# A long convolution by a two-stage Fourier transform: adjacent PSUM writes in the inverse, and a last stage in 32 × 32 tiles

## The chip, the cores and the metric

The kernel runs on one core of a Trainium2 chip. The time is the device time of one execution in microseconds, the median over several runs. The core has five engines with a queue of instructions each: TensorE (PE in the profile, and PEld for its weight loads), VectorE (DVE), ScalarE (ACT), GpSimd (POOL) and SyncE (SP), which here issues most of the DMAs. They wait for each other by semaphores only.

## The reference, cut to what matters

```python
x  = A_u                                    # 1 x 2048 x 512, bf16
xn = layernorm(x)
K  = real(sum over n of C * exp(dt*A*l) * dt*B)      # a filter of length 2048 for each of 512 channels
y  = irfft(rfft(xn, 4096) * rfft(K, 4096))[:2048]    # a causal convolution along the sequence
s  = y + xn * Dskip
g  = silu(xn + scatter_add(one row, a small gated MLP of that row))
return x + s * g
```

The convolution of 2048 positions for 512 channels is most of the work. The change touches only its last part: the product of the two spectra, the inverse transform, and the final `x + s * g`.

## The kernel before

The transform of length 4096 is done as two stages of small dense transforms on TensorE. A frequency is k2 + 64·k1 (32 values of k2, 64 of k1), a position is l1 + 64·l2 (64 values of l1, 32 of l2). Channels are split in two halves `h` of 256, and a half into four groups `q` of 64 channels `m`.

First come the layer norm, the forward transform of the input (`useq`, `useq2`), which goes through a DRAM scratch `scr_u`, and the generation of the filters from the parameters (`kgen_*`), a long chain on DVE. `kgen_kx` (L1057, stage kx1 for the second half) ends with KX, the filter at 640 sample points. Then, for each half:

- `load_u` (L1117) brings the spectrum of the input back into `UU[h]`, with the (real, imaginary) pair of k1 on the 128 partitions and `[t, q, k2, m]` along them; t = 1 is the same with the two parts swapped. For the second half the t = 1 copy is made by 8 copies on DVE or ScalarE (L1130, L1131).
- `spec` (L1137): for each of 16 pairs of k2, ten matmuls of 256 columns turn KX into the filter's spectrum in a PSUM bank (two banks alternate), `evac` copies it to `KF`, and DVE multiplies. For `h = 0` one instruction of 128 × 1024 multiplies UU in place. For `h = 1` four instructions of 128 × 256 write the products to another buffer `Y1`, whose innermost index is four channels.
- `inv_a` (L1160): the first inverse stage, from k1 to l1. Eight operations `x8` take eight channels m each; a channel is two matmuls (t = 0, 1) whose weights are the 128 values (q, k2) of that channel and whose 128 moving columns are the tables FA1 and FA2. The output of a channel goes to every fourth float of a bank (`pr.a.reshape(2, 128, 4)[i // 4, :, i % 4]`). Two pairs of banks alternate. Four copies of 64 partitions × 512 then bring (q, k2) × (part, l1) × m into `C`, so that the part lies on the upper or lower half of the partitions beside two of the four q, and the channels are adjacent.
- `fin_h` (L1203): the second inverse stage, from k2 to l2, and the end. For each l1 and q a matmul with 128 rows: the weights are a 128 × 32 table `FB` that holds zeros for the other q of the pair, the moving operand is 64 columns of C. The four values of l1 that lie 16 apart go to the four column strips of 32 (position `(0, 32 * a)`). ScalarE copies a group of rows to TB, DVE multiplies TB by G and adds it to XR (the input rows), and, for the second half only, four DMAs store the rows. The groups are 4, 4, 4, 4 values of l1 for `h = 0` and 4, 4, 4, 2, 2 for `h = 1`. In the last four rows a small matmul with VM (4 rows, table E127) first writes a correction.

`ldg` loads G (2 MB from scratch), `fpre` applies SiLU to it in four instructions of 128 × 2048 on ScalarE; `ldz` loads FB (1 MB), `ldr` the input rows XR.

In the program the order is spec0, inv0, loads and fpre, fin_h(0), spec1, inv1, fin_h(1). What each engine does in which order, though, is written out by hand: every operation has a number in the order of the program, the table `ORDER` lists the numbers for each of the five engines, and `_Graph.schedule` and `emit` only add the waits that follow from reads and writes. An operation made by `flex` or `evac` can stand in ScalarE's or in DVE's list. The `cost` arguments don't act in this kernel, since the order is given. In the old table fin_h(0) stands on TensorE in four pieces between the last spec1 operations and those of inv1 and its last piece behind inv1.

Of the kernel before, what the change touches and what calls it, by code (L numbers as in the profile page):

```python
# [340 lines left out]
def tables():  # L341
# [28 lines left out]
    FZ = np.zeros((2, 2, 32, 64, 2, 32))  # L370
    for q in range(2):
        FZ[:, q, :, :, q] = FB.transpose(2, 0, 1, 3)
    FB = FZ.reshape(128, 64, 2, 32)
# [6 lines left out]
        9 8 10 3-4 19 14 13 20 16 15 216 18 212 17 214 148 144 149-150 146 102 97 100 151 147 101 99 143 142 96 145 95 98 155 157 154 156 152-153 222  # L380
        224 218 220 226 228 230 232 236 238 234 240 250 252 242 254 316 256 258 321 260 708 264 262 326 331 709 336 268 341 270 266 346 710 351 711
        713-714 278 712 851 808 804 806-807 803 805 1006 1005 1004 1014 1016 1015 1025 1028 1026 1003 1052 1017 1027 1038 1051 1041 1040 1039""",
    scalar="""
        2 6 5 7 12 11 21 53-54 22 29 55 26 25 30 24 27 57-59 46 450 440 425 34 31 33 444 38 446 435 48 426 452 454 443 424 37 442 439 430 136 449 88
# [4 lines left out]
        592 579 597 578 575 340 338 500 598-599 570 628 577 590 587 574 588 600 345 343 514 576 520 581 348 518 350 595 586 522 596 582 524 584 572  # L389
        528 530 532 534 672 716 719 722 725 639 728 731 643 641 734 737 645 743 740 749 746 755 686 688 761 752 690 758 692 854 698 696 764-765 771  # L390
        700 769-770 776 775 704 777 781-782 786 811-812 789 792 790 879 810 873 794 891 801 885 809 897 802 915 909 797 927 921 939 933 951 823 945
        830 957 959-960 837 963 969 968 972 975 977 980 984 983 989 988 992 848 993 1000 1011 1022 1035 1048 1053-1054""",
    vector="""
        0-1 211 105 103 106 113 104 111 66 71 28 112 107 109 23 117 56 110 62-63 108 118 68 114 65 116 115 64 61 119 36 67 60 70 69 120 32 72 121 73
        122 74 123 75 84 124 76 125 77 126 78-79 127 131 80 128 81 129 82 130 132 83 133-134 85 137-139 86 135 140-141 87 91 90 92-93 89 94 161 164
        159 167 170 173 362 360 364 179 359 367 283 368 184-185 361 186 369 363 373 457 374 188 379 456 376 459 380 190 458 191-193 460 462 385 195
        461 388 464 463 197 466 198-200 465 375 467-468 202 469-472 386 473 205 474 476 475 210 477-478 274-275 479-482 309 484 488 485 506 486-487
        490 489 505 483 503 491-492 244 247 494 493 507 498 245 508 330 496 509-510 246 335 249 203 511-512 603 606 604 607 605 609 516 608 610-611
        671 613 612 615 614 616-617 619 618 673 621 630 620 622-623 625 624 626-627 526 629 631 633 632 272 635 276 634 277 674 636-637 646-647 649
        648 650-654 656 655 658 657 535 660 659 662 661 664 663 676 666 665 675 668 667 670 669 678 677 679-680 682 681 684 683 729 741 726 732 717  # L400
        747 735 744 762 720 738 723 759 753 750 756 857 694 853 766-767 855 859 772 774 706 858 702 852 707 779 784 780 787 785 867 791 871 861 856
        862-863 796 814 880-881 870 883 865 882 868 864 818 875 869 816 876 795 894 892 874 877 815 903 895 817 905 887 906 886 889 888 799 898 800
        900-901 899 893 912 904 913 910 930 911 907 925 929 924 922 916 941 940 942 918 917 923 934 931 919 928 943 937 953 955 954 952 936 824 935
        946 948 947 949 825 831-832 958 964 962 965 967 970 974 973 979 978 982 985 987 990 994 838 995 839 849-850 1001-1002 1012-1013 1023-1024
        1049-1050 1036-1037""",
    gpsimd="""
        447 390 389 536-537 42 39 41 40 43-44 594 279""",
    tensor="""
        45 47 158 160 163 166 162 169 165 172 168 171 175 178 174 181 49 177 282 51 180 183 286 187 290 280 189 294 284 194 298 196 288 302 201 292
        204 306 296 206-209 310 300 213 215 217 304 219 221 223 308 225 227 229 231 314 312 233 235 319 317 237 324 239 322 241 243 327 497 329 495  # L410
        332 501 334 499 337 339 515 344 251 253 255 519 342 513 349 347 257 259 517 261 263 521 525 523 527 529 531 533 265 267 269 271 715 718 721
        724 638 727 730 642 640 733 736 644 742 739 748 745 754 685 687 760 751 689 757 691 697 695 693 763 768 699 773 705 701 703 778 783 860 866
        788 813 793 878 872 798 890 884 902 896 914 908 926 920 938 932 950 819-822 944 826-829 956 961 833-836 966 840 842 841 843-845 971 976 981
        986 991 846-847 996-999 1007-1010 1018-1019 1031 1020-1021 1032 1029-1030 1033-1034 1044-1045 1042-1043 1046-1047""",
# [7 lines left out]
def build(nc, A_u, A_A_re, A_A_im, A_B_re, A_B_im, A_C_re, A_C_im, A_log_dt, A_Dskip,  # L422
# [52 lines left out]
    with g.ctx:  # L475
# [73 lines left out]
        C = apart("C", RM, RM2, [2, 64, 64])  # L549
        Y1 = g.buf("Y1", RQ0, [2, 16, 4, 32, 4], BF16)  # L550
# [29 lines left out]
        def cost(eng, v, rate):  # L580
            return FIX[eng] + v.n * rate
# [43 lines left out]
        def evac(out, in_):  # L625
            g.op(AC, lambda e: e.activation(out=out.ap, in_=in_.ap, func=ACT.Copy), w=[out], r=[in_], cost=cost(AC, out, 0.71) + 80,  # L626
                 alt=(DV, lambda e: e.tensor_copy(out=out.ap, in_=in_.ap), cost(DV, out, 1.05) + 95))  # L627

        def evac_a(out, in_):
            g.op(AC, lambda e: e.activation(out=out.ap, in_=in_.ap, func=ACT.Copy), w=[out], r=[in_], cost=cost(AC, out, 0.71))  # L630
# [506 lines left out]
        def spec(h, kps, fd, k0):  # L1137
            uu, kx = UU[h], KX[h]
            for n_, kp in enumerate(kps):
# [11 lines left out]
                if h == 0:  # L1151
                    uv = uu(uu.a[:, :, 2 * kp:2 * kp + 2].reshape(2, 4, 128))
                    tt(DV, uv, uv, kf(bc(kf.a[None], (2, 4, 128))), ALU.mult)
                else:
                    for kk in range(2):
                        for t in range(2):
                            k2 = 2 * kp + kk
                            tt(DV, Y1(Y1.a[t][:, :, k2].transpose(1, 0, 2)), uu(uu.a[t, :, k2].reshape(4, 16, 4)), kf(kf.a[:, 64 * kk:64 * kk + 64].reshape(4, 16, 4)), ALU.mult)
# [22 lines left out]
        inv_a(0)  # L1181
        g.stage = "ldz"
# [17 lines left out]

        nt = 0

        def fin_h(h):  # L1203
            nonlocal nt
            g.stage = f"fin{h}"
            for kb, (r0, nr) in enumerate(((0, 4), (4, 4), (8, 4), (12, 4)) if h == 0 else ((0, 4), (4, 4), (8, 4), (12, 2), (14, 2))):
                pr = PP[0 if h == 0 else kb % 2]
                bk = [PB[(0 if h == 0 else 2 * (kb % 2)) + k] for k in range(2)]
                blk = lambda q: bk[q // 2](bk[q // 2].a[64 * nr * (q % 2):64 * nr * (q % 2) + 64 * nr])
                for q in range(4):  # L1210
                    if r0 >= 12:
                        mm([(blk(q), CB(cb("E127")[0:128], 0, 4), VM(VM.a.reshape(4, 4, 2, 64)[r0 - 12:r0 - 12 + nr, q, h], 0, 4), q % 2 == 0, None, None)], 160)
# [81 lines left out]
```

## Time and profile before

| what | value |
|---|---|
| median of 3 runs | 220.25 us (219.12 to 220.3) |
| profiled execution | 220.46 us |
| its span, first to last instruction | 218.6 us |
| mean granted TensorE clock | 0.813 |
| copies of C | 30 on DVE, 34 on ScalarE |
| stores | 18 on SP, 2 on ScalarE |

A row of the profile names an engine, a line of the kernel (often that of a helper: L647 is every matmul, L626 and L627 every `evac` on ScalarE and on DVE, L598 every product of tensors), the buffers as out<-in, the shape as partitions × elements, and a count. In rows that group instructions, busy time and the mean duration in ns follow, then the idle time of the engine just before them and what ended it. In rows by time, the first number is the start in us from the start of the span, the second the length from the first start to the last end. In a table by stretches each engine has its busy time and number of instructions, then come the granted clock, the share of the DMA engines and GB/s. PB is any PSUM bank, and 128*64 on a matmul is rows times columns of the weights.

### The profile page before, as it was taken

How to read it: one execution, taken by the hardware profiler on the slowest of the kernel's cores; microseconds unless marked ns; L12 is line 12 of the kernel's file. 1: busy time of each engine (PE TensorE's matmuls, PEld its weight loads, DVE VectorE, ACT ScalarE, POOL GpSimd, SP SyncE). 2: the span in 40 equal slices, each digit the busy share in tenths (PEclk: the TensorE clock that was granted, in tenths of full speed). 3: DMA queues.
4: the chain of work that ended last, by engine and by line, in shares of the span. 5: the costliest groups of instructions: out<-in, count | busy, mean ns of one | idle time of the engine just before them, and what ended most of it. 6: DMA issues, size and time to landing. Idle time of an engine off the chain costs nothing.

```text
span 218.6 us, 6958 instructions
## 1 busy us (share of the span) xinstructions
PE 166.0 (76%) x2995; PEld 134.7 (62%) x2995; DVE 189.4 (87%) x408; ACT 161.3 (74%) x318; POOL 13.8 (6%) x17
## 2 busy tenths in 40 slices
PE   0150787799868768879957499989999997999440
PEld 0140676573654346657746488889889886988330
DVE  3999988998999999999999999476779999767970
ACT  2899999999999999999722144464689977556630
POOL 2021430000000000000000620000000000000000
PEclk9995555555965559999988799997999999999755
DMA  6990579700455896969999972059980000000076
GB/s 216 396 374 0 138 142 200 294 3 0 151 178 175 232 352 177 308 179 264 310 286 213 363 294 108 3 126 390 208 240 3 3 0 4 3 0 3 3 199 187
DMA packets 21142, 36.76 MB, mean 168 GB/s; under 512 B 1944, under 2 KB 16888, under 8 KB 20088
## 3 DMA queue, kind: packets, MB, share of 16 engines
q1 hardware_dynamic: 20120, 35.60, 54.2%
q10 hardware_dynamic: 960, 0.72, 1.0%
q8 instruction: 23, 0.38, 0.7%
q14 instruction: 7, 0.06, 0.1%
q0 software_dynamic: 32, 0.00, 0.0%
HBM read 25.83 MB, written 8.39 MB: 157 GB/s over the span
## 4 chain that ended last, share of the span: by engine, by line
PE 41%; DVE 35%; ACT 13%; issue 5%; DMA 2%; SPq 0%; DVEq 0%
PE PB L647 41%; DVE TT L598 8%; DVE QQ L598 8%; DVE Y L598 4%; DVE GG L598 3%; ACT E L593 2%; DMA X<-in_A_u_dram 2%; DVE ST L760 2%; ACT AU L626 2%; ACT TB L593 2%; ACT SL L593 2%; DVE LST L616 1%; ACT XT L626 1%; DVE QQ L1024 1%; ACT QQ L593 1%
## 5 line engine op out<-in xcount | busy, mean ns | idle before, releaser
L647 PE MATMUL PB<-KX,FD 128*128 128x256 bf16 x320 | 38.7, 281 | 0.0
L647 PEld LDWEIGHTS PB<-KX,FD 128*128 128x128 bf16 x320 | 31.6, 101 | 5.8 <-ACT KX L626 0.4
L647 PE MATMUL PB<-QQ,GG 128*20 128x42 bf16 x1024 | 25.0, 263 | 9.7 <-DVE QQ L598 5.2
L647 PEld LDWEIGHTS PB<-QQ,GG 128*20 128x20 bf16 x1024 | 21.4, 124 | 13.5 <-issue 6.8
L627 DVE CAST C<-PB 64x512 bf16<-64x512 f32 x30 | 20.7, 689 | 9.5 <-PE PB L647 8.2
L626 ACT ACTIVATE C<-PB 64x512 bf16<-64x512 f32 x34 | 20.1, 592 | 11.9 <-PE PB L647 10.7
L626 ACT ACTIVATE KF<-PB 128x512 bf16<-128x512 f32 x29 | 17.3, 598 | 13.7 <-PE PB L647 12.9
L598 DVE TENSOR_TENSOR TT<-GG,MB 128x2048 bf16<-128x2048 bf16 (+3 forms) x32 | 24.3, 787 | 0.3
L593 ACT ACTIVATE QQ<-TH 128x256 bf16<-128x256 f32 x64 | 22.5, 427 | 0.0
L593 ACT ACTIVATE E<-AR 128x256 bf16<-128x256 f32 x64 | 22.3, 426 | 0.0
L598 DVE TENSOR_TENSOR QQ<-QQ,E 128x1024 bf16<-128x1024 bf16 (+2 forms) x16 | 19.6, 1252 | 0.0
L647 PE MATMUL PB<-CB,XZN 32*128 32x64 bf16 x256 | 15.8, 327 | 4.4 <-ACT AU L626 3.5
L647 PEld LDWEIGHTS PB<-CB,XZN 32*128 32x128 bf16 x256 | 12.8, 203 | 7.0 <-ACT AU L626 5.0
L647 PE MATMUL PB<-CB,UU 128*128 128x128 bf16 x128 | 17.0, 338 | 0.0
L626 ACT ACTIVATE KE<-PB 128x336 bf16<-128x336 f32 x13 | 6.0, 464 | 13.7 <-PE PB L647 13.7
L647 PE MATMUL PB<-AU,F2U 64*128 64x256 bf16 x128 | 12.6, 342 | 4.4 <-ACT UST L626 3.6
L647 PEld LDWEIGHTS PB<-CB,UU 128*128 128x128 bf16 x128 | 15.7, 185 | 0.4 <-issue 0.2
L598 DVE TENSOR_TENSOR GG<-TT 128x1024 bf16<-128x1024 bf16 (+3 forms) x38 | 15.1, 434 | 0.4
L647 PE MATMUL PB<-CB,Y 128*128 128x128 bf16 x128 | 14.6, 313 | 1.1 <-DVE Y L598 1.1
L626 ACT ACTIVATE AU<-PB 128x1024 bf16<-128x1024 f32 x14 | 14.2, 1041 | 0.5 <-PE PB L647 0.5
L647 PEld LDWEIGHTS PB<-CB,Y 128*128 128x128 bf16 x128 | 13.5, 137 | 1.6 <-DVE Y L598 1.2
L598 DVE TENSOR_TENSOR Y<-UU,KF 128x256 bf16<-128x256 bf16 x64 | 14.0, 283 | 0.4 <-ACT KF L626 0.3
(133 smaller groups left out, 287.5 us busy)
## 6 DMA issues: line engine op xcount, KB each, us to landing
FD<-c_fd SPq DMA_DIRECT2D x4, 1280.0 KB, 7.6
scr_u<-UST SPq DMA_DIRECT2D x8, 512.0 KB, 5.2
UU<-scr_u SPq DMA_DIRECT2D x2, 2048.0 KB, 15.4
XZN<-XN SPq DMA_DIRECT2D x16, 128.0 KB, 4.2
scr_g<-XN SPq DMA_DIRECT2D x4, 512.0 KB, 7.2
UU<-scr_u SPq DMA_DIRECT2D x2, 1024.0 KB, 11.3
XR<-in_A_u_dram SPq DMA_DIRECT2D x4, 512.0 KB, 14.6
G<-scr_g SPq DMA_DIRECT2D x1, 2048.0 KB
```

Source lines behind the costliest of these rows:

```text
L593: g.op(AC, lambda e: e.activation(out=out.ap, in_=in_.ap, func=func, **kw), w=[out], r=r, cost=cost(AC, out, 0.71), table=table, tokr=tokr ...
L598: g.op(eng, lambda e: e.tensor_tensor(out=out.ap, in0=a.ap, in1=b.ap, op=op), w=[out], r=[a, b], cost=cost(eng, out, rate))
L616: g.op(eng, lambda e: e.scalar_tensor_tensor(out=out.ap, in0=a.ap, scalar=x, in1=b.ap, op0=op0, op1=op1), w=[out], r=r, cost=cost(eng, out ...
L626: g.op(AC, lambda e: e.activation(out=out.ap, in_=in_.ap, func=ACT.Copy), w=[out], r=[in_], cost=cost(AC, out, 0.71) + 80, alt=(DV, lambda ...
L627: alt=(DV, lambda e: e.tensor_copy(out=out.ap, in_=in_.ap), cost(DV, out, 1.05) + 95))
L647: ins = e.matmul(o_.ap, lhsT=l_.ap, rhs=r_.ap, start=st, stop=sp, **kw)
L760: g.op(DV, lambda e, b=b: e.bn_stats(ST6(ST6.a[b]).ap, X0(X0.a[b]).ap), w=[ST6(ST6.a[b])], r=[X0(X0.a[b])], cost=620)
L1024: lambda e: e.tensor_scalar(out=out.ap, in0=in_.ap, scalar1=-1.0, scalar2=None, op0=ALU.mult), cost(DV, out, 0.3))
```

## The change

The program becomes: spec0, inv0, spec1, inv1, loads and fpre, then one last stage for both halves.

- In `inv_a` a channel's output goes to 128 adjacent floats, for both halves from UU; `Y1` is gone, and in `spec` both halves multiply UU in place.
- One copy per `x8` brings all 128 partitions × 1024 elements to C and swaps channel and (part, l1) on the way: it reads PSUM with a step of 128 floats and writes eight adjacent channels. Only the last one of the second half is split in two. C is now `[h, part, l1, m]` on partitions (q, k2), and its second half lies where UU0 was.
- The second inverse stage is undivided by half: `FB` is the bare table, repeated on four strips of 32 partitions. For each l1, part and q a matmul of 32 rows × 32 columns of weights and 128 moving columns (both halves) goes to position `(32 * q, 32 * a)`, and the two parts accumulate. Each q has its own bank. There are 512 such matmuls, as there were of the old kind.
- Row groups of the last stage are 2, 4, 4, 2, 2, 2 values of l1 for both halves together, each with two copies, products and adds of 128 × 256 nr elements; the last product of all is taken by DVE straight from PSUM in two pieces. There are 24 stores instead of 20, 2 of them on ScalarE.
- `ORDER` is a new table throughout. The work before spec0's inverse is the same set of operations in another order, and some movable ones change engine. TensorE now does the end of the second half's filters with the first two inverse operations between, then inverse operations of the first half between those of spec1, the last two of them behind spec1, then inv1 and the last stage (group 1 before group 0). ScalarE has the copies of inv0's operations 0, 1, 6, 7 and of inv1's 0 to 5 and half of 7, DVE the others. Three of the four SiLU instructions stand on ScalarE between spec1's copies 0 and 5, the fourth before copy 6. SP loads G, FB and XR in this order instead of XR, G, XR, XR, FB, XR.

```diff
-    FZ = np.zeros((2, 2, 32, 64, 2, 32))
-    for q in range(2):
-        FZ[:, q, :, :, q] = FB.transpose(2, 0, 1, 3)
-    FB = FZ.reshape(128, 64, 2, 32)
+    FB = np.tile(FB, (4, 1, 1, 1))
...
-        C = apart("C", RM, RM2, [2, 64, 64])
-        Y1 = g.buf("Y1", RQ0, [2, 16, 4, 32, 4], BF16)
+        C = apart("C", RM, RQ0, [2, 64, 64])
...
-                if h == 0:
-                    uv = uu(uu.a[:, :, 2 * kp:2 * kp + 2].reshape(2, 4, 128))
-                    tt(DV, uv, uv, kf(bc(kf.a[None], (2, 4, 128))), ALU.mult)
-                else:
-                    for kk in range(2):
-                        for t in range(2):
...
+                uv = uu(uu.a[:, :, 2 * kp:2 * kp + 2].reshape(2, 4, 128))
+                tt(DV, uv, uv, kf(bc(kf.a[None], (2, 4, 128))), ALU.mult)
...
-                        lst.append((pr(pr.a.reshape(2, 128, 4)[i // 4, :, i % 4]), uu(uu.a[t, :, :, m].reshape(128)) if h == 0 else Y1(Y1.a[t, m // 4, :, :, m % 4].reshape(128)), CB(cb(("FA1", "FA2")[t])), t == 0, t == 1, None))
-                mm(lst, 60 if h else 92)
-                for tq in range(2):
-                    for ri in range(2):
-                        evac(C(C.a[h, tq, :, 8 * x8:8 * x8 + 8].reshape(64, 2, 4).transpose(1, 0, 2), 64 * ri, 64), pr(pr.a.reshape(2, 2, 64, 4)[:, ri], 64 * tq, 64))
+                        lst.append((pr(pr.a[128 * i:128 * i + 128]), uu(uu.a[t, :, :, m].reshape(128)), CB(cb(("FA1", "FA2")[t])), t == 0, t == 1, None))
+                mm(lst, 92)
+                for i in range(2) if h == 1 and x8 == 7 else (None,):
+                    cv = C.a[h, :, :, 8 * x8:8 * x8 + 8].reshape(128, 8)
+                    pv = pr.a.reshape(8, 128).transpose(1, 0)
+                    evac(C(cv if i is None else cv[:, 4 * i:4 * i + 4]), pr(pv if i is None else pv[:, 4 * i:4 * i + 4]))
...
+        SET = ((0, 1), (2, 3))
+        for kb, (r0, nr) in enumerate(((0, 2), (2, 4), (6, 4), (10, 2), (12, 2), (14, 2))):
+            prs = [PP[k] for k in SET[kb % 2]]
+            blk = lambda q: PB[2 * SET[kb % 2][q // 2] + q % 2].part(512 * (2 * SET[kb % 2][q // 2] + q % 2), [2, nr, 64])
...
+            for b4 in range(nr):
+                lst = []
+                for ri in range(2):
+                    for a in range(4):
+                        for q in range(4):
+                            k_ = blk(q)
                             l1 = 16 * a + r0 + b4
-                            lst.append((bk[q // 2](bk[q // 2].a[c0:c0 + 64], 32 * a, 32), FB(FB.a[l1, q % 2]), C(C.a[h, q // 2, l1]), r0 < 12, None, (0, 32 * a)))
-                    mm(lst, 15)
+                            lst.append((k_(k_.a[:, b4], 32 * a, 32), FB(FB.a[l1, ri], 32 * q, 32), C(C.a[:, ri, l1], 32 * q, 32), ri == 0 and r0 < 12, None, (32 * q, 32 * a)))
+                mm(lst, 15)
+            for qp in range(2):
...
+                if r0 == 14 and qp:
+                    for q in range(2):
+                        tt(DV, t_(t_.a[n_ * q:n_ * q + n_].reshape(2, 64 * nr)), prs[qp](prs[qp].a[512 * q:512 * q + n_].reshape(2, 64 * nr)), G0(gv[2 * q:2 * q + 2]), ALU.mult)
+                else:
+                    evac_a(t_(t_.a[0:2 * n_].reshape(2, n_)), ps)
...
```

More of the change, by code (lines that the diff above doesn't have):

```diff
@@ L415 @@
+        910 922 921 924-926 940 937-939 941-942""",
 )
@@ L1181, in build @@
         inv_a(0)
+        g.stage = "spec1"
+        load_u(1)
+        spec(1, range(16), FD, 0)
+        g.stage = "inv1"
+        inv_a(1)
+        g.stage = "fin"
         g.stage = "ldz"
@@ L1230, in fin_h @@
-                if h:
-                    for a in range(4):
-                        store(_dma_rows(out, 8192 * a + 512 * r0, [[32768, 32], [1, 512 * nr]]), XR(XR.a[r0:r0 + nr].reshape(-1), 32 * a, 32), 32 * 1024 * nr, eng=SP if r0 < 14 or a < 2 else AC)
-        fin_h(0)
-        g.stage = "spec1"
-        load_u(1)
-        spec(1, range(16), FD, 0)
-        g.stage = "inv1"
-        inv_a(1)
-        fin_h(1)
+                ps = prs[qp](prs[qp].a.reshape(2, 512)[:, :n_])
+                gv = G0.a[2 * qp:2 * qp + 2, :, r0:r0 + nr].reshape(4, 64 * nr)
@@ L1241, in build @@
+                tt(DV, xv, t_(t_.a[0:256 * nr].reshape(4, nr, 64)), xv, ALU.add)
+            for a in range(4):
+                store(_dma_rows(out, 8192 * a + 512 * r0, [[32768, 32], [1, 512 * nr]]), XR(XR.a[r0:r0 + nr].reshape(-1), 32 * a, 32), 32 * 1024 * nr, eng=SP if r0 < 14 or a < 2 else AC)
         g.schedule(ORDER)
```

82 lines of the change are left out of this document (31 added, 51 removed), and 10 rows, old and new, of the table scalar.

## The prediction

> **What bounds the kernel now.** I read the page's busy row first, then a table by stretches of the span from 144.5 us on (the work before it is left as it is, only reordered), then the chain of work that ended last.
>
> ```profile
> span 218.6 us, 6958 instructions
> PE 166.0 (76%) x2995; PEld 134.7 (62%) x2995; DVE 189.4 (87%) x408; ACT 161.3 (74%) x318; POOL 13.8 (6%) x17
> ...
> core 0: us, PE busy (x) PEld busy (x) DVE busy (x) ACT busy (x) POOL busy (x), PEclk, DMA share, GB/s
> ...
> 147.00:150.50 3.50, 3.50 (x20) 3.50 (x19) 1.50 (x3) 0.61 (x2) 0.00 (x0) 0.51 0.93 346
> 150.50:159.50 9.00, 9.00 (x98) 8.01 (x97) 6.73 (x12) 6.21 (x12) 0.00 (x0) 1.00 1.00 279
> 159.50:170.00 10.50, 10.50 (x95) 9.64 (x93) 9.43 (x22) 9.98 (x10) 0.00 (x0) 1.00 0.34 95
> 170.00:185.80 15.80, 14.70 (x248) 12.39 (x246) 15.34 (x63) 12.85 (x19) 0.00 (x0) 1.00 0.01 3
> 185.80:201.80 16.00, 16.00 (x240) 14.73 (x244) 11.49 (x17) 9.36 (x16) 0.00 (x0) 1.00 0.01 2
> 201.80:204.10 2.30, 0.35 (x36) 0.26 (x38) 2.21 (x4) 2.09 (x3) 0.00 (x0) 1.00 0.00 0
> 204.10:213.30 9.20, 5.24 (x264) 3.85 (x264) 7.43 (x13) 4.22 (x5) 0.00 (x0) 0.55 0.46 126
> ```
> ```profile
> 119.08 3.93 issue
> ...
> 144.52 28.71 PE PB L647 x264
> ...
> 185.80 16.00 PE PB L647 x228
> ...
> 203.35 0.60 ACT C L626
> ```
>
> DVE leads the whole-span row, but from 144.5 to 201.8 TensorE is busy almost without a gap, and the chain runs over it in two long pieces. Between them DVE carries the chain from 173.3 to 185.8 through the Y products. So the stretch of 57.3 us is bound by the pace of matmuls, with some DVE in the middle; from 204 us on it is a pipeline of evacuation, two DVE passes and stores.
>
> **The pace of the inverse.** It has 256 matmuls of 128 columns, 128 in each half.
>
> ```profile
> 146.73 4.05 PE L647 MATMUL PB<-CB,UU 128*128 128x128 bf16 x20
> 192.83 8.95 PE L647 MATMUL PB<-CB,Y 128*128 128x128 bf16 x80
> 169.74 12.38 PE L647 MATMUL PB<-KX,FD 128*128 128x256 bf16 x110
> ...
> L647 PEld LDWEIGHTS PB<-CB,UU 128*128 128x128 bf16 x128 | 15.7, 185 | 0.4 <-issue 0.2
> L647 PEld LDWEIGHTS PB<-CB,Y 128*128 128x128 bf16 x128 | 13.5, 137 | 1.6 <-DVE Y L598 1.2
> ...
> 57.89 0.80 PEld L647 LDWEIGHTS PB<-CB,XZN 32*128 32x128 bf16 x16 [0.73 <-ACT AU L626]
> 57.89 0.94 PE L647 MATMUL PB<-CB,XZN 32*128 32x64 bf16 x16 [0.64 <-ACT AU L626]
> ```
>
> With 128 columns the inverse takes 8.95/80 = 0.112 us each, as long as the spectrum stage with 256 columns (12.38/110 = 0.1125). At the granted clock of 0.51 it takes 4.05/20 = 0.20. So it costs two clocks a column, and it isn't the weight load that sets it: loads from UU last 185 ns and from Y 137 ns, at one pace. What both have in common and the spectrum stage has not is the output with a step of 4 floats. Written adjacent, 128 columns should take half, 0.056 us. But then the weight load is next: U lies with a step of 64 elements in both halves after the change. The row with such weights and few columns is XZN: 16 loads, in pairs on two row strips, take 0.80 us from the first start to the last end, and their matmuls 0.94. With a latency of some 0.2 us taken off, the seven steps between pairs are 0.086 by the loads and 0.106 by the matmuls. I take 0.093 us for the new pace, nearer to the loads; the ends are 0.056 (load hidden) and 0.112 (nothing gained).
>
> [...]
>
> **The change part by part**, made against the profiled execution (220.46 us for a span of 218.6, so 1.86 us around it; the median of the runs is 220.25).
>
> ```profile
> L627 DVE CAST C<-PB 64x512 bf16<-64x512 f32 x30 | 20.7, 689 | 9.5 <-PE PB L647 8.2 <-ACT C L626 0.7
> L626 ACT ACTIVATE C<-PB 64x512 bf16<-64x512 f32 x34 | 20.1, 592 | 11.9 <-PE PB L647 10.7
> L598 DVE TENSOR_TENSOR Y<-UU,KF 128x256 bf16<-128x256 bf16 x64 | 14.0, 283 | 0.4 <-ACT KF L626 0.3
> L598 DVE TENSOR_TENSOR UU<-UU,KF 128x1024 bf16<-128x1024 bf16 x16 | 9.9, 688 | 3.8 <-ACT KF L626 3.8
> L626 ACT ACTIVATE AU<-PB 128x1024 bf16<-128x1024 f32 x14 | 14.2, 1041 | 0.5 <-PE PB L647 0.5
> L627 DVE CAST AU<-PB 128x1024 bf16<-128x1024 f32 x2 | 2.4, 1221 | 0.9 <-PE PB L647 0.9
> L593 ACT ACTIVATE G<-G 128x2048 bf16<-128x2048 bf16 x4 | 7.6, 1925 | 0.0
> ...
> 12.50 0.57 ACT L626 ACTIVATE AR<-PB 128x512 f32<-128x512 f32 x1
> 144.78 1.86 PE L647 MATMUL PB<-CB,KE 128*64 128x80 bf16 x28
> 167.56 0.68 DVE L598 TENSOR_TENSOR V<-PB,K2R 4x512 bf16<-4x512 f32 x1
> 169.78 0.34 DVE L605 TENSOR_SCALAR VM<-V,CF 4x512 bf16<-4x512 bf16 x1
> ```
>
> *Copies and products.* 64 half-height copies (20.7 + 20.1 = 40.8 us of two engines) become 15 of 1024 elements and two of 512: 10 on ScalarE at 1.04, 5 on DVE at 1.22, the halves 0.59 and 0.69, in all 17.8 us. 64 Y products (14.0) become 16 in place (9.9). They now read PSUM with a step of 128 floats; the AR copy does so on ScalarE at 0.57 us for 512, no dearer than the C copies. DVE has no such row: none lower than 1.22, and twice that as the upper end, of which only the last two copies (2 us) would be on the path. I take no extra. DVE and ScalarE then have some 29 us of work each where TensorE has 48, so their time in the middle costs nothing; what is late next is TensorE itself.
>
> *The middle on TensorE, from 144.5.* The end of the filter stage (kx1) about 4.0 (40 matmuls on KE at 1.86/28, 2.7, and a tail of some 35 smaller ones); the first 32 inverse matmuls, at half clock as now, half of 0.20 each, 3.2; the other 224 × 0.093 = 20.8; 160 spectrum matmuls × 0.1125 = 18.0. Of waits I count 2.4: 0.7 before the first inverse matmul, which needs the last product of the first half, and 1.7 where ScalarE's spectrum copies stand behind three SiLU passes (3 × 1.92) and DVE products behind those. G is now the first of SP's loads of that group, so SiLU needn't wait long for it; FB and XR, moved behind it, are needed only after 194. Then 1.0 for the reordered part before 144.5: DVE, which carries much of the chain there, gives 14 movable operations of 8.0 us to ScalarE and takes 21 of 9.6 us from it. The fetch stall of 3.93 us at 119 I leave in. The inverse so ends at 144.5 + 1.0 + 4.0 + 3.2 + 20.8 + 18.0 + 2.4 = 193.9 instead of 201.8, and its last copy, split over two engines, 0.9 later, at 194.8 (now 203.95).
>
> *The end.* All of the last stage is behind the inverse now, not half of it. Its first tile matmul waits for the last copy of the inverse; all that TensorE has left is queued behind it, and ScalarE, DVE and SP wait for that in turn, so nothing of the stage is covered any more.
>
> ```profile
> 204.08 1.45 PE L647 MATMUL PB<-C,FB 128*32 128x64 bf16 x128 [1.95 <-ACT C L626]
> 204.92 2.09 ACT L593 ACTIVATE TB<-PB 128x1024 bf16<-128x1024 f32 x2 [0.98 <-PE PB L647]
> 205.20 0.69 DVE L598 TENSOR_TENSOR XR<-TB,XR 128x1024 bf16<-128x1024 bf16 x1
> 205.97 0.69 DVE L598 TENSOR_TENSOR TB<-TB,G 128x1024 bf16<-128x1024 bf16 x1
> 212.41 0.42 DVE L598 TENSOR_TENSOR TB<-TB,G 128x512 bf16<-128x512 bf16 x1
> 212.86 0.42 DVE L598 TENSOR_TENSOR XR<-TB,XR 128x512 bf16<-128x512 bf16 x1
> 215.85 0.89 SPq L664 DMA_DIRECT2D out_dram<-XR  x2
> ```
>
> The first group (128 tile matmuls) takes 1.45 if the pace of the present 32-column tiles holds, its copy 1.02; DVE starts 2.65 us after the last copy, and the V and VM work (0.68 + 4 × 0.34) lies inside that. DVE then has 8 passes of 1024 at a pitch of 0.71 (205.20 to 205.97 and on), 15 of 512 at 0.42, and two products of 256 out of PSUM, about 0.42 each (an estimate, a quarter of the 1.22 copy and some overhead): 12.8 us. ScalarE (8.2) and TensorE (512 × 0.0113 = 5.8) fit beside it; each group frees its banks early enough. SP issues a store in 0.45. Its first needs both adds of the second group, DVE's seventh pass (2.65 + 3 × 0.71 + 4 × 0.42 = 6.5); its 22 take 9.9 and nearly keep up with DVE. After the last add three remain on SP (1.35), and the last lands 1.9 us later (now 216.74 to 218.6). Sum 2.65 + 12.8 + 1.35 + 1.9 = 18.7, against 14.65 now (203.95 to 218.6): the end grows by 4.05. Span 194.8 + 18.7 = 213.5, time **215.4 us**.
>
> A tile matmul of 32 × 32 has no row. Four column strips run at 0.0113 (1.45/128) with 64 columns; 128 columns on the same four strips would be 0.023, sixteen tiles at once half of 0.0113. One after another they would be 0.056. The nearest row gives 0.0113; at 0.023 the first group is 1.5 us later and the rest still hides. [...]
>
> **Rivals.**
> *The load hides (0.056).* For it: at equal pace the UU load is 48 ns longer than Y's and costs nothing. Against it: the XZN row, where the pair's pace is above its columns' time. Six operations of the first half end 0.59 us sooner each (16 × 0.037); in the second the ScalarE copy (1.04 and a latency of 0.16) limits them, 8 × 0.29. That is 5.8 less: 209.6 us.
> *The adjacent write does nothing (0.112), the change not doing what it says.* For it: no row has stepped weights with an adjacent output. Then 224 × 0.019 = 4.3 more: 219.7 us.
> *The tiles run one after another.* Place: the end, behind the inverse. For it: no row shows row and column strips together. Against: pairs of row strips and four column strips do overlap (rows above). 512 × 0.056 = 28.7, after which a copy, a product and an add (1.5) and the stores (3.2): the end takes 33.4 instead of 18.7, 230 us. It decides from 0.037 us a tile matmul on: below that the end is within 23.8 us after 194.8 and the kernel not slower than now.
>
> **How the numbers follow.** Forecast 0.56, own range 213 to 218 (waits of the middle, half a microsecond to either side in the end, a fetch stall that moves); load hidden 0.14; write does nothing 0.22, spread by 2 us around 219.7; tiles in series 0.08. A measurement tells about 0.5% (1.1 us) from no change, so below 219.15 counts as faster: 0.54 + 0.14 + 0.08 = 0.76; within: 0.02 + 0.09 = 0.11; above 221.35: 0.05 + 0.08 = 0.13. The range of 209 to 221.5 leaves out the serial tiles, the top of the second rival and the lower tail of the first, 0.18.
>
> **What would show it.** Right: inverse matmuls of 0.09 us with LDWEIGHTS back to back; 17 C copies of about 1.04 and 1.22; inverse ending near 194; DVE busy without gaps for 13 us behind it; SP's last store 1.4 us after the last add. Wrong: an inverse at 0.109 or 0.056; spectrum matmuls at 0.21 behind a clock of 0.5 (each costs 0.1); tile matmuls above 0.03 us; a fetch stall in the middle; a DVE copy of C well above 1.22; or the filter stage ending more than 2 us from 145.5.

## The result, and the profile after

The changed kernel takes **214.02 us** (median of 4 runs, 213.15 to 215.56) where the kernel before took 220.28 beside it (219.12 to 221.11): a ratio of 0.973, 95% interval 0.966 to 0.980. The prediction was 215.4, with a range of 213 to 218. The profiled execution took 213.15 us, with a span of 211.1.

The page's first lines: TensorE, DVE and ScalarE all have less to do (before 166.0, 189.4 and 161.3 us).

```profile
span 211.1 us, 6855 instructions
PE 157.4 (75%) x2991; PEld 127.7 (60%) x2991; DVE 174.7 (83%) x354; ACT 146.9 (70%) x286; POOL 11.8 (6%) x17
```

The chain of work that ended last (start, length, what):

```profile
115.25 4.80 issue
120.05 23.12 PE PB L640 x466
143.70 45.57 PE PB L640 x482
189.29 0.70 DVE C L620
190.04 1.74 PE PB L640 x172
191.78 2.00 issue
```

From 143.70 us to the last inverse matmul the chain is one piece on TensorE, where before it was two with DVE between. Behind the last copy and 172 tile matmuls there is a stall of 2.00 us that the kernel before did not have there. The stretches, with the columns of the table by stretches shown of before:

```profile
143.70:146.30 2.60, 2.60 (x41) 2.56 (x42) 2.57 (x6) 2.58 (x3) 0.00 (x0) 1.00 0.84 252
146.30:149.70 3.40, 3.40 (x33) 3.33 (x32) 3.28 (x6) 1.22 (x2) 0.00 (x0) 0.51 0.98 414
149.70:189.30 39.60, 39.60 (x416) 37.02 (x414) 22.75 (x34) 24.11 (x26) 0.00 (x0) 1.00 0.32 82
189.30:211.10 21.80, 8.44 (x521) 5.35 (x520) 13.62 (x31) 8.32 (x12) 0.00 (x0) 0.61 0.38 99
```

TensorE is busy for every one of the 45.6 us, and DVE and ScalarE for little more than half of the long stretch. The inverse and spectrum stages by time, then the groups by form:

```profile
146.24 3.64 PE L640 MATMUL PB<-CB,UU 128*128 128x128 bf16 x32
163.78 11.08 PE L640 MATMUL PB<-KX,FD 128*128 128x256 bf16 x100
174.70 14.56 PE L640 MATMUL PB<-CB,UU 128*128 128x128 bf16 x160
```
```profile
L640 PE MATMUL PB<-CB,UU 128*128 128x128 bf16 x256 | 24.6, 261 | 0.0
L640 PEld LDWEIGHTS PB<-CB,UU 128*128 128x128 bf16 x256 | 24.1, 199 | 0.4 <-ACT KX L619 0.3
L619 ACT ACTIVATE C<-PB 128x1024 bf16<-128x1024 f32 x10 | 10.2, 1024 | 6.1 <-PE PB L640 6.1
L620 DVE CAST C<-PB 128x1024 bf16<-128x1024 f32 x5 | 6.1, 1225 | 13.0 <-PE PB L640 12.9
```

An inverse matmul takes 14.56/160 = 0.091 us (0.112 before), with the loads busy for almost as long as the matmuls, and the copies (1.024 us on ScalarE, 1.225 on DVE) cost what the AU copies of the same size cost in this trace (1.013 and 1.224). So the time went this way:

| part of the span | before | after | difference |
|---|---|---|---|
| up to kx1 | 144.52 | 143.70 | -0.8 |
| kx1 to the last inverse matmul | 57.3 | 45.6 | -11.7 |
| on to the end of the last copy of C | 2.15 | 0.7 | -1.5 |
| from there to the end | 14.65 | 21.1 | +6.5 |
| span | 218.6 | 211.1 | -7.5 |

Of the 11.7, 7.0 are the inverse itself (17.0 + 14.6 us of matmuls before, 24.6 now); some 3.0 are the 256 tile matmuls that stood inside this stretch and have moved to the end (three pieces of 0.73 and two of 0.42); and 1.1 is the wait for the last Y product. Some 0.6 is not accounted for.

### The profile page after: what moved, and what is told of

Same layout as the page of the kernel before. It is cut to its first block, busy times and chain, and to the rows that moved or that the text cites. A ratio compares the mean times of both kernels' runs of the same rounds, so it can differ in the third digit from the quotient of the medians.

```text
span 211.1 us, 6855 instructions
## 1 busy us (share of the span) xinstructions
PE 157.4 (75%) x2991; PEld 127.7 (60%) x2991; DVE 174.7 (83%) x354; ACT 146.9 (70%) x286; POOL 11.8 (6%) x17
## 4 chain that ended last, share of the span: by engine, by line
DVE 42%; PE 39%; issue 5%; DMA 5%; ACT 3%; SPq 3%; DVEq 0%
PE PB L640 39%; DVE TT L591 12%; DVE QQ L591 8%; DVE GG L591 4%; DVE ST L753 4%; DMA XZN<-XN 3%; SPq L657 3%; DMA X<-in_A_u_dram 2%; DVE TB L591 2%; DVE XR L591 1%; DVE LST L609 1%; DVE UST L620 1%; ACT XN L778 1%; ACT TB L623 1%; DVE MB L947 1%
## 5 line engine op out<-in xcount | busy, mean ns | idle before, releaser
L619 ACT ACTIVATE KF<-PB 128x512 bf16<-128x512 f32 x25 | 14.8, 597 | 27.1 <-PE PB L640 26.5
L640 PE MATMUL PB<-QQ,GG 128*20 128x42 bf16 x1024 | 23.9, 263 | 4.5 <-DVE QQ L591 4.5
L640 PEld LDWEIGHTS PB<-QQ,GG 128*20 128x20 bf16 x1024 | 21.1, 123 | 8.0 <-DVE QQ L591 5.3
L591 DVE TENSOR_TENSOR UU<-UU,KF 128x1024 bf16<-128x1024 bf16 x32 | 20.6, 685 | 5.7 <-ACT KF L619 5.7
L640 PE MATMUL PB<-CB,UU 128*128 128x128 bf16 x256 | 24.6, 261 | 0.0
L640 PEld LDWEIGHTS PB<-CB,UU 128*128 128x128 bf16 x256 | 24.1, 199 | 0.4 <-ACT KX L619 0.3
L620 DVE CAST C<-PB 128x1024 bf16<-128x1024 f32 (+1 forms) x6 | 6.8, 1136 | 13.2 <-PE PB L640 13.1
L640 PEld LDWEIGHTS PB<-CB,XZN 32*128 32x128 bf16 x256 | 12.9, 202 | 5.9 <-ACT AU L619 3.1
L619 ACT ACTIVATE C<-PB 128x1024 bf16<-128x1024 f32 (+1 forms) x11 | 10.8, 985 | 8.0 <-PE PB L640 8.0
L640 PE MATMUL PB<-CB,XN 128*64 128x128 bf16 x128 | 7.5, 291 | 10.4 <-ACT XN L778 9.0
L619 ACT ACTIVATE UST<-PB 128x1024 bf16<-128x1024 f32 x14 | 14.2, 1023 | 0.9 <-PE PB L640 0.9
L640 PEld LDWEIGHTS PB<-CB,XN 128*64 128x64 bf16 x128 | 6.0, 154 | 11.1 <-ACT XN L778 9.1
```

What stands on the lines that cost most here:

```text
L591: g.op(eng, lambda e: e.tensor_tensor(out=out.ap, in0=a.ap, in1=b.ap, op=op), w=[out], r=[a, b], cost=cost(eng, out, rate))
L640: ins = e.matmul(o_.ap, lhsT=l_.ap, rhs=r_.ap, start=st, stop=sp, **kw)
```

## The experiments

All start from the changed kernel ("after") unless a text says otherwise. As times are measured beside the kernel before on the same chip, the ratio to it is what is compared: after has 0.973.

### The writes stepped again

```diff
-lst.append((pr(pr.a[128 * i:128 * i + 128]), ...
+lst.append((pr(pr.a.reshape(2, 128, 4)[i // 4, :, i % 4]), ...
-evac(C(cv), pr(pr.a.reshape(8, 128).transpose(1, 0)))
+evac(C(cv.reshape(128, 2, 4)), pr(pr.a.reshape(2, 128, 4).transpose(1, 0, 2)))
```

> After with one thing undone: the inverse's matmuls write PSUM every fourth element again, the 17 merged copies stay (they read runs of four). Theory (the inverse became faster because its writes became adjacent): TensorE's pace in the inverse goes from the 91 ns of after back to about 109 to 112 ns, 256 x 0.019 = about 4.5 us more, 217.5 to 219.5 us. Rival (the gain is from the merged copies and the new order, the writes do nothing): the pace stays at 91 ns and the time at 214.0 within 0.7 us. The copies themselves should stay near 1.02 (ScalarE) and 1.22 us (VectorE) by both.

219.24 us, ratio 0.996 (0.992 to 0.999). In the rows by time:

```profile
177.54 17.63 PE L640 MATMUL PB<-CB,UU 128*128 128x128 bf16 x160
```

17.63/160 = 0.110 us, and the copies take the same 1.02 and 1.22. The theory holds: by the ratios, this one edit undone gives back 5.1 of the 6.0 us.

### The weights adjacent

This kernel leaves out the gathering of a channel's 128 values: each inverse matmul takes 128 neighbours of U as its weights. Count and size of everything stay.

```diff
-uu(uu.a[t, :, :, m].reshape(128))
+uu(uu.a[t].reshape(-1)[128 * m:128 * m + 128])
```

> After, but the inverse's 128-column weights are read from 128 adjacent elements of U in place of every 64th; the output is then another permutation of the work, the same count of everything. Theory (after's 91 ns per matmul is the load of weights at a stride): the pace falls to the plain 56 ns in the first inverse, and to about 65 ns in the second, where a copy of 1.04 us per 16 matmuls on ScalarE is the floor: 128 x 0.035 + 128 x 0.026 = 7.8 us less, 205.5 to 209 us. Rival (the 91 ns is from the write into PSUM, or from the copies): pace 91 ns and time within 1 us of 214.0.

207.77 us, ratio 0.944 (0.941 to 0.948). One row of the first inverse, the loads, and the second inverse:

```profile
157.00 1.06 PE L640 MATMUL PB<-CB,UU 128*128 128x128 bf16 x16
...
174.33 8.61 PE L640 MATMUL PB<-CB,UU 128*128 128x128 bf16 x128 [0.22 <-ACT C L619]
```
```profile
L640 PEld LDWEIGHTS PB<-CB,UU 128*128 128x128 bf16 x256 | 16.1, 103 | 2.1 <-ACT C L619 1.3 <-ACT KX L619 0.3
```

In an operation of 16, the last end lies some 0.2 us behind the last start (an estimate from 1.58 for 16 in after at 0.091 each), so the first inverse goes at about 0.057. The second takes 8.61/128 = 0.067 and now waits for copies, as foreseen. So after's 0.091 is the load at a step of 64 elements. In us a matmul, the write at a step of 4 floats is 0.110, this load 0.091, and plain columns are 0.057, about half of the first.

### Both

This kernel has the two edits above together, and so leaves out the same gathering.

```diff
+lst.append((pr(pr.a.reshape(2, 128, 4)[i // 4, :, i % 4]), uu(uu.a[t].reshape(-1)[128 * m:128 * m + 128]), ...
```

> Both edits of the two kernels ahead: writes at every fourth element, weights adjacent. Theory (each matmul takes the longer of its write and of the next load, not their sum): pace 109 to 112 ns, as with stepped weights, 217.5 to 219.5 us. Rival (the two costs add): 91 - 35 + 19 = 75 ns, about 210 us.

219.87 us, ratio 0.994 (0.990 to 0.998).

```profile
178.94 17.63 PE L640 MATMUL PB<-CB,UU 128*128 128x128 bf16 x160
```

The same 17.63 us as with stepped weights. A matmul here takes the longer of its write and the next load, not their sum. This is why, before, a slow load cost nothing and made the write look like the whole price.

### The copies in four pieces, on one engine

```diff
-evac(C(cv), pr(pv))
+for j in range(2):
+    for p in (0, 64):      # four instructions of 64 x 512, one engine
+        copy(C(cv[:, 4 * j:4 * j + 4], p, 64), pr(pv[:, 4 * j:4 * j + 4], p, 64))
```

> After with every merged copy of the inverse done in four instructions of 64 rows x 512 on the same engine, as many as before the change (64 and not 17, some 23 us more busy time), the second inverse's copies alternating between ScalarE and VectorE. Theory (the copies' saving lies beside TensorE and is worth nearly nothing): pace in the inverse stays at 91 ns, the last half copy costs 0.6 us more: 214 to 216 us. Rival (the merged copies are the gain): the inverse becomes paced by its copies, over 219 us.

226.94 us, ratio 1.032 (1.029 to 1.036). The theory fell by 11 us: with four pieces a copy is not beside TensorE. Two stretches of the trace (a span of 222.8, 11.7 more than after) grew. From kx1 to the last 160 inverse matmuls it takes 35.2 us instead of 31.0: the pieces stand ahead of the spectrum's copies on ScalarE and DVE, and TensorE waits 1.46 us for a copy of KX and 0.97, 0.37 and 0.32 for three of KF. The 160 matmuls take 22.3 instead of 14.6. Some of their rows by time:

```profile
178.90 7.25 ACT L629 ACTIVATE C<-PB 64x512 bf16<-64x512 f32 x12 [0.80 <-PE PB L657]
...
183.78 1.94 PE L657 MATMUL PB<-CB,UU 128*128 128x128 bf16 x16 [0.72 <-ACT C L629]
...
186.20 1.78 PE L657 MATMUL PB<-CB,UU 128*128 128x128 bf16 x16 [0.48 <-ACT C L629]
...
188.02 2.40 ACT L629 ACTIVATE C<-PB 64x512 bf16<-64x512 f32 x4 [1.88 <-PE PB L657]
188.61 1.63 PE L657 MATMUL PB<-CB,UU 128*128 128x128 bf16 x16 [0.62 <-DVE C L634]
...
197.70 1.95 PE L657 MATMUL PB<-CB,UU 128*128 128x128 bf16 x16 [1.40 <-DVE C L634]
```

The first three copies stand back to back on ScalarE (twelve pieces in 7.25 us), and there the operations of 16 matmuls start 2.4 us apart because that engine is full. From 188.61 to 197.70 the copies alternate between the engines, and four operations still start 2.27 us apart on the average instead of 1.45, though both engines have idle time (ScalarE 1.88 us ahead of its copy). Each operation waits for the copy of the one two places earlier, which had the same PSUM pair. For the second inverse two explanations were left: this ring of two pairs, or the engines' time.

### The copies in four pieces, on two engines

```diff
+for p in (0, 64):          # rows 0-63 on ScalarE, 64-127 beside it on DVE
+    two instructions of 64 x 512
```

Only the first seven copies of the second inverse.

> After with the first seven copies of the second inverse each done in four instructions of 64 x 512, two on ScalarE (rows 0 to 63) beside two on VectorE (rows 64 to 127); the first inverse keeps its merged copies. Theory (what cost 12.9 us when all four were on one engine was the ring of two PSUM pairs: 1.45 us of matmuls, 2.4 to 2.8 us of copy and 0.5 us of signals per pair before it is free again): 1.45 + 1.4 + 0.5 = 3.35 us for two groups, 1.67 a group where TensorE needs 1.45, 7 x 0.22 = 1.5 us more, 215 to 216.5 us. Rival (the engines' busy time is what cost): as many copy instructions as in the second inverse of the kernel with four on one engine, that inverse again takes 22 us where after's takes 14.6, over 219 us.

213.46 us, ratio 0.965 (0.958 to 0.973), no dearer than after.

```profile
174.24 15.09 PE L657 MATMUL PB<-CB,UU 128*128 128x128 bf16 x160
...
184.83 1.07 ACT L629 ACTIVATE C<-PB 64x512 bf16<-64x512 f32 x2 [0.53 <-PE PB L657]
184.83 1.30 DVE L634 CAST C<-PB 64x512 bf16<-64x512 f32 x2 [0.30 <-PE PB L657]
```

28 pieces instead of 7 copies lengthen the second inverse by 0.5 us (15.09 instead of 14.56), so in the second inverse it was how long a copy holds its pair, and not the sum of the busy time. The 1.5 us that I had expected were too many. A copy may last until its pair is wanted again: two operations of 1.45 less its own 1.45 less some 0.3 of signals (an estimate from the kernel with Y below: two operations there take 2.20 us, of which 0.91 are matmuls and 1.02 the copy), about 1.15. The merged copy on ScalarE (1.02) fits, 2.4 doesn't, and 1.30 is over by a little. So half of the 23 us of copying that the change saves, the half beside the second inverse, is worth almost nothing as busy time. For the other half, beside the first inverse and the spectrum, this isn't shown: those copies stay merged here, and in the kernel ahead that stretch took 4.2 us longer.

### The first inverse in one piece

```diff
-tensor: ... 705 767 788 791 769 794 797 773 803 800 771 806 ... 833 775 777 836 ...
+tensor: ... 705 767 769 771 773 775 777 788 791 794 797 803 800 806 ... 833 836 ...
```

The lists of ScalarE and DVE follow: the copies of the first inverse ahead of those of the spectrum.

> After with the first inverse's eight groups one behind the other ahead of the second spectrum on every engine, where after strews groups three to eight among the spectrum's matmuls. Theory (the interleaving only fills TensorE's wait while ScalarE does SiLU, 1 to 2 us): 214.5 to 216.5 us. Rival (the new order is the gain of the change): the 6 us come back, 219 us or more.

219.25 us, ratio 0.996 (0.991 to 1.001). The rival was right on the size: the place of six inverse operations in the order is worth 5.0 us by the ratios, as much as the adjacent write. What TensorE waited for from 144 to 195 us (total, times, longest):

```profile
PE PB L640 <- DVE KF L620: 1.6, 2, 0.8
PE PB L640 <- DVE UU L591: 1.5, 1, 1.5
PE PB L640 <- ACT KF L619: 0.7, 1, 0.7
```

After has none of the three. 2.3 us are spectrum matmuls waiting for copies while ScalarE is at SiLU, and 1.5 the second inverse waiting for the spectrum's last product. Together they are 3.8 us; the last 1.2 of the 5.0 are not accounted for. In after, inverse operations of the first half stand in both gaps, the last two of them behind the spectrum.

### SiLU beside the first inverse

```diff
-scalar: ... 704 702 789 860 862 861 804 859 807 ... 834 776 778 837 ...
+scalar: ... 704 702 860 862 861 859 789 792 795 ... 831 834 837 ...
```

The first inverse stays in one piece; its copies 2 to 7 go to DVE, all copies of the spectrum to ScalarE.

> The first inverse in one piece ahead of the second spectrum, as in the kernel that took 5.2 us more than after, but with ScalarE's four SiLU instructions and their table load ahead of the spectrum's copies, beside the first inverse, all eight rear copies of that inverse on VectorE but the first two, and all the spectrum's copies on ScalarE. Theory (those 5.2 us were SiLU's 8.6 us standing between the spectrum's copies, with TensorE waiting; any order that puts SiLU beside the inverse does): TensorE is unbroken from kx1 to the end of the inverse again, 213.5 to 215.5 us. Rival (an inverse in one piece is itself slower, by its ring of two PSUM pairs): 217 us or more.

216.32 us, ratio 0.982 (0.973 to 0.990). 3 of the 5 us are back, though the interval overlaps that of after. What is left of the three waits:

```profile
PE PB L640 <- DVE UU L591: 1.4, 1, 1.4
```

The waits for the spectrum's copies are gone, and the gap behind the spectrum, which no place of SiLU can fill, stays. The theory, all of it SiLU, had the larger part only; of the rival's ring nothing is seen. As the edit moves copies between the engines too, it doesn't show that SiLU's place alone did it.

### Four neighbours together: Y again

To the kernel with SiLU early. Since Y lies over U of the first half, the first inverse has to be in one piece.

```diff
-tt(DV, uv, uv, kf(...), ALU.mult)                      # 128 x 1024 in place
+four of 128 x 256 into Y1[t, m // 4, q, k2, m % 4]      # second half, as before the change
-uu(uu.a[t, :, :, m].reshape(128))
+Y1(Y1.a[t, m // 4, :, :, m % 4].reshape(128))           # second inverse
```

> That kernel, with the second half's products written as before the change: four instructions for each of 16 steps (64, not 16) into Y, where four neighbouring columns lie together, and the second inverse's weights read from Y at a step of 4 elements in place of 64. Theory (the load of weights is the bound, and its price depends on the step): pace of the second inverse between 56 and 91 ns, middle 75: 2.0 us less than the kernel with SiLU early, 211.5 to 213.5 us; the copies' ring (68 ns in the kernel with adjacent weights) does not bind. VectorE's 64 x 0.22 = 14 us of products fit beside the spectrum's 18 us. Rival (a stride costs the same whatever it is): the pace stays at 91 ns and the time at the kernel with SiLU early, or above it by what the products add.

213.15 us, ratio 0.968 (0.956 to 0.981), 3.2 less than the kernel with SiLU early. The intervals of the two ratios overlap, so it is the trace that carries the point: the 128 matmuls took 11.77 us there and take 8.6 here. The products, and the second inverse by time:

```profile
L1136 DVE TENSOR_TENSOR Y<-UU,KF 128x256 bf16<-128x256 bf16 x64 | 14.4, 289 | 3.4 <-ACT KF L620 3.4
```
```profile
178.53 1.98 PE L641 MATMUL PB<-CB,Y 128*128 128x128 bf16 x32 [1.62 <-DVE Y L1136]
...
180.74 2.00 PE L641 MATMUL PB<-CB,Y 128*128 128x128 bf16 x32 [0.22 <-ACT C L620]
```

32 matmuls start every 2.2 us, 0.069 each, and the gap between is a wait for a copy. At a step of 4 elements the load is at most that. So the Y products that the change removed were not only a cost: beside an adjacent write they buy a faster load.

### Every product at a step of 128

```diff
-Y1 [t, m // 4, q, k2, m % 4]
+Y1 [t, m, q, k2]
```

> As the kernel with Y, but Y laid out so that the second inverse's 128 weights are adjacent; VectorE then writes every product at a step of 128 elements. Theory: pace 68 ns (bound by the copies' ring, as where the weights were adjacent), 128 x 0.023 = 2.9 us less than the kernel with SiLU early, if the strided writes cost VectorE no more than 0.27 us a product (64 x 0.27 = 17 us beside the spectrum's 18); at 0.33 us a product VectorE has 21 us, sets the spectrum's pace, and the gain is gone. 211 to 214.5 us. Rival (product layout free, load not the bound): as the kernel with Y within 0.7 us.

271.17 us, ratio 1.232 (1.221 to 1.244). A miss by 57 us:

```profile
L1136 DVE TENSOR_TENSOR Y<-UU,KF 128x256 bf16<-128x256 bf16 x64 | 72.9, 1514 | 0.5 <-ACT KF L620 0.5
```

By busy time it is 72.9/64 = 1.14 us a product instead of 14.4/64 = 0.23, five times as long for 256 elements, because each result now lies 256 bytes from the last and not in runs of four. I had allowed 0.27 to 0.33.

### Stores on a second queue

```diff
-eng=SP if r0 < 14 or a < 2 else AC
+eng=SP if a < 2 else PO if r0 < 14 else AC
```

The end of after, which these two experiments are about: DVE's first product, its two idle gaps and its last addition, and SP's stores.

```profile
192.50 0.69 DVE L591 TENSOR_TENSOR TB<-TB,G 128x1024 bf16<-128x1024 bf16 x1 [0.76 <-ACT TB L623]
...
195.31 0.76 DVE L591 TENSOR_TENSOR TB<-TB,G 128x512 bf16<-128x512 bf16 x2 [1.40 <-ACT TB L623]
...
197.62 11.63 SPq L657 DMA_DIRECT2D out_dram<-XR  x22
...
198.76 0.69 DVE L591 TENSOR_TENSOR TB<-TB,G 128x1024 bf16<-128x1024 bf16 x1 [0.57 <-ACT TB L623]
...
205.23 0.75 DVE L591 TENSOR_TENSOR XR<-TB,XR 128x512 bf16<-128x512 bf16 x2
```

> After with 10 of SyncE's 22 output stores (the upper two row quarters of the first five groups) issued by GpSimd's queue instead. In after, SyncE issues its 22 stores without a break from 197.62 to 209.25 us, while the last addition ends at 205.98. Theory (the end is set by SyncE's issue of 0.53 us a store): SyncE has 12 stores, 6 us, and is done with all but the last two when the last addition ends: 205.98 + 0.9 + 1.9 of landing = 208.8 of span where after has 211.1, 2.3 us less, 211.0 to 212.5 us. Rival (the end is set by VectorE's additions or by the transfers themselves): 214.0 within 0.7 us.

212.30 us, ratio 0.965 (0.960 to 0.970), a span of 209.8.

```profile
197.55 9.91 SPq L657 DMA_DIRECT2D out_dram<-XR  x12
...
205.43 0.75 DVE L591 TENSOR_TENSOR XR<-TB,XR 128x512 bf16<-128x512 bf16 x2
```

The last addition ends at 206.18 (after 205.98), so DVE's end is untouched; SP is done 1.28 us behind it (after 3.27). Of the expected 2.3 us, 1.3 appear in the span and 1.7 in the median, whose intervals overlap; the trace is what carries the point. Of the 1.0 us missing in the span, 0.2 is the later addition, 0.4 is SP's tail (1.28 instead of 0.9; one store of the fifth group stands last in its list), and 0.4 is the landing of the last store (2.3 instead of 1.9).

### The group of two rows first

```diff
-tensor: ... 863 881-884 869-870 ...      sync: ... 880 879 877 893 891-892 878 894 ...
+tensor: ... 863 869-870 881-884 ...      sync: ... 879-880 877-878 893 891-892 894 ...
```

> After with the group of two rows (the first in the output) ahead of the group of four on every engine and queue, nothing else changed. In after, TensorE stalls 2.0 us at the 172nd tile matmul, in the middle of the group of two, and the first store starts at 197.62. Theory (the stall comes at a fixed place in the instruction stream, and the stores wait for it only because the group of two lies across it): the stall stays at about the 172nd matmul, the group of two is through before it, the first store starts near 194, SyncE's 22 x 0.53 us end near 205.7, and VectorE's 13 us of work from 191.5 on set the end, near 209 of span, 1.5 to 2.5 us less: 211.5 to 212.7 us. Rival (the stall belongs to the group of two, a wait for a copy of C or for a load): it moves to the start of the stage with that group and the time stays at 214.0 within 0.7 us or grows.

214.01 us, ratio 0.970 (0.961 to 0.980): no gain. Its chain, and its stores by time:

```profile
189.92 1.74 PE PB L640 x172
191.66 1.87 issue
193.52 1.34 PE PB L640 x128
194.87 2.38 issue
```
```profile
192.97 15.83 SPq L657 DMA_DIRECT2D out_dram<-XR  x22
...
205.25 0.75 DVE L591 TENSOR_TENSOR XR<-TB,XR 128x512 bf16<-128x512 bf16 x2
```

The mechanism was right and the gain was not. The stall comes after 172 tile matmuls whichever group is first, so it belongs to a place in the stream of instructions and not to a group; the first store starts 4.65 us earlier. But 128 matmuls on there is a second stall, 2.38 us. In after it was 0.60 at this place, soon after a wait of 1.26 for a copy; that the wait hid the rest of it fits, but isn't shown. DVE's last addition ends at 206.0 in both, and SP again has a backlog behind it. Here a store that started early didn't move the last one.

### Together

The kernel with Y, stores on GpSimd's queue (with the fifth group's last store ahead of the sixth's), and three PSUM pairs for the second inverse:

```diff
-pr = PP[2 + x8 % 2]
+pr = PP[1 + x8 % 3] if h else PP[2 + x8 % 2]     # copies of h = 1 alternate ScalarE, DVE
```

> The kernel with Y (SiLU beside the first inverse, products in Y with four neighbours together) with two more edits: ten of SyncE's stores on GpSimd's queue, the last of the fifth group ahead of the sixth group's; and three PSUM pairs in a ring for the second inverse, its copies alternating between ScalarE and VectorE. Theory: the second inverse of the kernel with Y is bound by its ring of two (32 matmuls in 2.0 + 0.2 us, 69 ns each); with three pairs only the load is left, 56 to 65 ns, 0.5 to 1.5 us less; the stores take 1.7 us away as they did alone. 213.15 - 1.0 - 1.7 = 210.5, 209 to 211.5 us. Rival (VectorE's additions, which end at 206.0 in after with or without the other stores, hold the end, and the ring is not what binds): 211.5 to 213 us.

**209.96 us**, ratio 0.952 (0.947 to 0.958): faster than both kernels, its interval clear of after's, and in the range foreseen.

```profile
179.76 7.34 PE L641 MATMUL PB<-CB,Y 128*128 128x128 bf16 x128 [1.62 <-DVE Y L1136]
```
```profile
187.89 1.74 PE PB L641 x173
189.63 1.85 issue
```

7.34/128 = 0.057 us: with three pairs, and the copies on two engines, neither ring nor load is left, and the second inverse goes at the pace of its columns. The two edits to its copies were not tried apart. The stall behind 173 tile matmuls is still there.

## Why the prediction was right, and where it was not

- **The write sets the pace before, the load after.** Right, and shown both ways: 0.110 with the write stepped, 0.091 with the load at a step of 64, 0.057 with neither. I took 0.093 from XZN, where the weights have the same step but a pair of loads of 32 rows goes together; no row said that such a pair costs what one load of 128 rows does, so being this close is in part luck. "Two clocks a column" is, in what the rows show, twice the spectrum's time for a column (0.112 us for 128 and 0.1125 for 256); a clock rate is in no row. Of the rivals, the hidden load (0.056) needs adjacent weights or a step of 4 (0.057 in both), and the write that does nothing (0.112) is refuted: with adjacent weights the write alone makes 0.110 of 0.057. The 0.16 us of latency in the first rival's sum is in no row; with adjacent weights the second inverse took 8.61/8 = 1.08 us an operation, where that sum had 1.20.
- **Copies and products off the path.** Right for after, but too simple. What I compared was busy time (29 us against 48). In the second inverse what decides is whether a copy is done when its PSUM pair comes round, and 1.02 us had little slack below the estimated 1.15. In the spectrum a copy also delays what is queued behind it on its engine (31.0 us became 35.2 with the copies in four pieces). Copies of 2.4 us, in both, cost 12.9. No extra cost of DVE reading PSUM at a step of 128 floats: right, 1225 ns, and 1224 for its AU copy, which reads adjacent floats.
- **Waits of the middle, 2.4 us.** The term that was mis-sized: TensorE had none there. I read the order table for SiLU and missed that inverse operations had been put into the gaps. The run without this interleaving shows 2.3 us of SiLU waits and 1.5 behind the spectrum, so waits of that size exist; the order removes them. The stretch was 2.8 shorter than predicted; most of the other 0.4 is the spectrum, 17.5 us instead of 18.0.
- **The reordered part, +1.0 us.** Not borne out: kx1 began 0.8 earlier, though the stall on its way grew from 3.93 to 4.80. But in the traces of other kernels here that share this part it began anywhere from 142.10 (the copies in four pieces on one engine) to 144.71 (SiLU early), so 0.8 between two traces doesn't show the part to be faster. I had called this stall a fetch stall; the profile says only "issue", and no run shows what it is. No run took this part by itself.
- **The end, 18.7 us.** Mis-sized the other way: 21.1. DVE started at 2.5 (2.65 predicted) and went on for 13.48 (12.8), with idle gaps of 1.40 and 0.57 in it behind the 2.00 us stall, and the tail on SP was 3.27 instead of 1.35. I had SP "nearly keep up"; it began a microsecond late at 7.6 behind the last copy, needs 11.63/22 = 0.53 a store and not 0.45 (the median is 0.43, but the longest take 1.07 and 1.17), and never caught up.
- **Tile matmuls.** Right: 1.74 us for 172, 0.010 each between the stalls, nothing in series. Over a piece with its stall, as in the kernel with the group of two first, it is (1.34 + 2.38)/128 = 0.029.

That the time came within 1.4 us of the forecast is in part luck, since the errors partly cancelled: -1.8 up to kx1, -2.8 in the middle, -0.2 at the copies and +2.4 at the end make the 2.4 us by which the span was shorter than predicted.

## What to carry to other kernels

Where two costs of a matmul hide each other, as the load of 0.091 us and the write of 0.110 did here, a cost seen to be free is only shorter than the one above it: take the price of the second from the nearest row before removing the first, and expect the gain to stop there. In these runs a copy out of PSUM was off the path only where it ended before its bank was wanted again (1.02 us did, 2.4 us did not), whatever the engines' busy shares said, and where nothing that TensorE needed soon was queued behind it on its engine (in the spectrum that cost 4.2 us). And work moved out of a full stretch to the end needs an account of every queue there, the stalls of TensorE (2.00 and 0.60 us) and the store queue (22 stores in 11.63 us) too: here 11.7 us were won and 6.5 of them paid back.

## What the runs showed of the hardware

- Loading 128 × 128 weights with 128 columns to hide behind costs 0.091 us a matmul at a step of 64 elements and no more than 0.057 at a step of 4, the same as with adjacent weights. No step between 4 and 64 was tried for these loads.
- A DVE product of 128 × 256 that writes runs of four elements takes 0.23 us, one that writes single elements 256 bytes apart 1.14.
- In the run of tile matmuls TensorE stalls after the 172nd (2.00 us in after) and 128 later, after the 300th (0.60 in after, 2.38 with the groups exchanged), at the same places whichever group is first. In the other kernels the first stall comes after the 169th to the 173rd. The profile calls it issue time. It counts 0.38 MB in 23 packets of one instruction queue, 16.5 KB each, and in after one of them moves at about 191.4 us, just ahead of the stall that starts at 191.78. Whether TensorE waits there for its instructions isn't shown: no run changed it.
- SP's 22 stores behind each other take 0.53 us each (11.63/22), GpSimd's ten in the last kernel 0.50 each (5.0 us in all), side by side with SP's.
